# Fewer, longer loads of q and v in an attention kernel, and its bias tiles asked for by GpSimd

## The chip, the cores and the metric

The kernel runs on one core of a Trainium2 chip. What counts is the time of one execution in microseconds of that core (device time); the median of the runs shown is compared. The engines are named as in the profile: PE is TensorE, PEld its weight loads, DVE VectorE, ACT ScalarE, POOL GpSimd, SP SyncE. SP computes nothing: in this kernel it issues the DMAs.

## What is computed

Attention over 4 batches, 8 heads, 576 rows and 64 columns a head, with a bias that a small network makes of the distance of query and key; then a mixture of 8 experts over the 2304 rows, each row with a weight from a Sinkhorn normalization:

```
scores = q @ k.T / sqrt(64) + bias[head]         # bias = relu(x @ w1 + b1) @ w2, x from the positions alone
attn   = softmax(scores)                          # with 1e-9 added to the sum
x      = attn @ v                                 # (4, 8, 576, 64), laid out as 2304 rows x 512
P      = exp(x @ w_gate), 8 times normalized over rows and columns
out    = sum over e of P[:, e] * (relu(x @ w1[e]) @ w2[e])     # 8 experts, 512 -> 1024 -> 512
```

## The kernel before

**Units.** The attention is cut into 16 units: one batch and two heads each (`units`, line 687; neighbouring batches run through the head pairs in opposite order, so that a unit may take over its neighbour's bias tiles). A unit's 576 rows are seen as 64 partitions of `R` = 9 rows each: row 9p + r lies with partition p. Query tiles t = 0 to 3 hold rows r = t and r = t + 4 (128 queries), tile 4 holds row 8 of both heads. A unit has five steps (`unit_steps`): two query tiles for each of two heads, then the next two, then tile 4.

**Loading a unit.** `u_load` asks for q in three DMAs (rows 0 to 3 into partitions 0 to 63, rows 4 to 7 into partitions 64 to 127, row 8 by itself) and for k in one. `u_vload` asks for v in four. All land in the rotating buffers `nat` (four). `u_cut` splits q and k into two f16 halves on ACT and DVE (`asplit`: ACT writes the high part, DVE the rest), `u_trans` turns them on PE into the bank `l1` and evacuates them into `qkT` by ACT, DVE and ACT; GpSimd then writes a copy with the partition halves swapped. `u_v` splits v into `vs`, and GpSimd writes its swapped copy. `b_load` asks for two bias tiles `bt` a unit, unless the unit before has the same heads.

**A step.** PE multiplies q and k into a score bank (`s`, two of them); DVE adds the bias, keeps the row's extreme and frees the bank (`sb`, the custom instruction); ACT takes the exponential (`sb<-sb,st`), then writes the high f16 half of the probabilities into `ah` (two buffers); DVE writes the low half; SP issues a DMA transpose of `ah` into `aT`; PE multiplies `aT` with `vs` (`pv`). Between these, PE works through pieces of expert 0 (`run_piece`, bank `l`).

**Order.** Within the attention every call is recorded (`Plan.record`), with a modelled cost, and what it reads and writes; `Plan.emit` replays the model and emits the instructions in the order of its start times. Each engine then works its own instructions off in that order; SP and GpSimd too. An instruction that waits holds up what stands behind it on its engine. For a DMA on SP the model takes 0.5 us of issuing, on GpSimd 1.05 (`Engine.transfer`, line 224). The steps loop `for n in range(NS + LAG + 1)` at line 1137 calls the loads some steps ahead through `hooks`. Behind the attention come gate, Sinkhorn and experts 1 to 7 (line 1194 on), planned by a second plan.

Of the kernel before, what the change touches and what calls it, by code (L numbers as in the profile page):

```python
# [10 lines left out]
F32 = mybir.dt.float32  # L11
# [7 lines left out]
P = 128  # L19
B, H, S, D = 4, 8, 576, 64  # L20
# [5 lines left out]
R = S // 64  # L26
# [244 lines left out]
def attention_sinkhorn_moe(ctx, tc, q, k, v, w1, b1, w2, wg, m1, m2, xm, xm4, xf, sel, out):  # L271
# [12 lines left out]
    vec, act, pool, pe, sync = (  # L284
        Engine(plan, e, n)
        for e, n in ((nc.vector, "dve"), (nc.scalar, "act"), (nc.gpsimd, "pool"), (nc.tensor, "pe"), (nc.sync, "dma"))
    )
# [62 lines left out]
    sc_bias = dram.tile([H, P, 2, S], F32, name="sc_bias")  # L350
# [62 lines left out]
    with ExitStack() as actx:  # L413
# [21 lines left out]
        nat, spl, uni, bst, wrk = places("nat", 4), places("spl"), places("uni", 2), places("bst", 2), places("wrk")  # L435
# [13 lines left out]
        def ps_s():  # L449
            return psA.tile([P, 1024], F32, name="ps_s", tag="s", bufs=2)  # L450
# [68 lines left out]
        for kind in range(1, 4):  # L519
            vec.scalar_tensor_tensor(  # L520
                out=wr,
# [8 lines left out]
            out=wa.rearrange("p g (j k) -> p (g j) k", j=4),  # L530
# [92 lines left out]
        def bias_step(between=()):  # L623
# [27 lines left out]
            out=w1r, in0=pw[:, H : H + 2], scalar1=s_wb[:, 0:1], scalar2=2.0**-11, op0=ALU.mult, op1=ALU.mult  # L651
# [5 lines left out]
            out=w2m,  # L657
# [22 lines left out]
        for i in range(2):  # L680
            r = slice(32 * i, 32 * i + 1)
# [5 lines left out]
        units = [(b, hp if b % 2 == 0 else NHP - 1 - hp) for b in range(B) for hp in range(NHP)]  # L687
        U = {}

        def nat_tile():  # L690
            return nat.tile([P, 10 * D], F32, name="nat", tag="nat")

        def ld(u):
            return sync

        def u_load(u):
            if u >= len(units):
                return
            b, hp = units[u]
            h0 = 2 * hp  # L700
            qn = nat_tile()[:, : R * D].rearrange("p (r d) -> p r d", d=D)
            src = q[b, h0 : h0 + 2].rearrange("h (p r) d -> p h r d", r=R)
            for i in range(2):
                hs = slice(64 * i, 64 * i + 64)
                ld(u).dma_start(
                    out=qn[hs, 0:8, :].rearrange("p (h c) d -> p h c d", h=2), in_=src[:, :, 4 * i : 4 * i + 4, :]
                )
            ld(u).dma_start(out=qn[:, 8, :], in_=q[b, h0 : h0 + 2].rearrange("h (p r) d -> (h p) r d", r=R)[:, 8, :])
            kn = nat_tile()[:, : R * D].rearrange("p (r d) -> p r d", d=D)
            ld(u).dma_start(out=kn, in_=k[b, h0 : h0 + 2].rearrange("h (p r) d -> (h p) r d", r=R))  # L710
            U[u] = dict(qn=qn, kn=kn)

        def u_cut(u):
# [9 lines left out]
        def u_vload(u):  # L723
            if u >= len(units):
                return
            b, hp = units[u]
            h0 = 2 * hp
            vn = nat_tile().rearrange("p (h c d) -> p h c d", h=2, c=5)
            vv = v[b, h0 : h0 + 2].rearrange("h (p r) d -> p h r d", r=R)
            for i in range(2):  # L730
                hs = slice(64 * i, 64 * i + 64)
                ld(u).dma_start(out=vn[hs, :, 0:4, :], in_=vv[:, :, 4 * i : 4 * i + 4, :])
                ld(u).dma_start(out=vn[hs, :, 4, :], in_=vv[:, :, 8, :])
            U[u]["vn"] = vn

        def u_v(u):
            if u >= len(units):
# [15 lines left out]
        def u_trans(u):  # L753
            if u >= len(units):
                return
            st = U[u]
            if u in (2, 3):
                qkT = xc[:, u - 2, : 27 * P].rearrange("p (n x) -> p n x", x=P)
            else:
                qkT = uni.tile([P, 27, P], F16, name="qkT", tag="qkT")  # L760
            qk = st.pop("qk").rearrange("p (i r) a d -> p i r (a d)", i=2)
            for i in range(3):
                ps = psA.tile([P, 1024], F16, name="ps_t", tag="l1", bufs=2).rearrange("p (r x) -> p r x", x=P)
                rows = [(i, r) for r in range(8)] if i < 2 else [(0, 8), (1, 8)]
                with plan.as_one():
                    for j, (a, r) in enumerate(rows):
                        pe.transpose(ps[:, j], qk[:, a, r], id16)
                if i == 0:
                    act.copy(qkT[:, 0:8], ps)
                elif i == 1:  # L770
                    vec.tensor_copy(qkT[:, R : R + 8], ps)
                else:
                    act.copy(qkT[:, : 2 * R].rearrange("p (i r) x -> p i r x", i=2)[:, :, 8], ps[:, 0:2])
            for i in range(2):
                pool.tensor_copy(qkT[64 * i : 64 * i + 64, 2 * R :], qkT[64 - 64 * i : 128 - 64 * i, :R])
            st.update(q=(qkT[:, :R], qkT[:, 2 * R :]), kT=qkT[:, R : 2 * R])

        def b_load(u, hh):

            if u and units[u][1] == units[u - 1][1]:  # L780
                U[u]["b", hh] = U[u - 1]["b", hh]
                return
            bt = bst.tile([P, 2, S], F32, name="bt", tag="bt")
            sync.dma_start(out=bt, in_=sc_bias[2 * units[u][1] + hh])
            U[u]["b", hh] = bt

        def b_tile(u, t, hh):
# [7 lines left out]
        for n in range(8):  # L795
            for m in (2 * n, 2 * n + 1):
                nm, _, i = qk_order[m]
# [9 lines left out]
        with plan.urgent():  # L807
# [6 lines left out]
            out=c8, in0=u_qk[:, 0:1], scalar=0.125, in1=u_qk[:, 1:2], op0=ALU.mult, op1=ALU.mult  # L814
# [7 lines left out]
            out=g, in0=g0, scalar=s_qk[:, 0:1], in1=s_qk[:, 1:2], op0=ALU.mult, op1=ALU.mult  # L822
# [25 lines left out]
        with plan.urgent():  # L848
            u_cut(0)
            u_trans(0)  # L850
# [49 lines left out]
        def scores(u, t, hh):  # L900
            ps = ps_s()
            kT = U[u]["kT"]
            kv = kT[:, 0:8, :].rearrange("p (r c) x -> p c r x", r=2)
            for a, qT in enumerate(U[u]["q"]):
                for c in range(2):
                    for h in (hh,) if t < 4 else (0, 1):
                        hs = slice(h * 64, h * 64 + 64)
                        lhs = qT[:, 4 * h + t, :] if t < 4 else qT[:, 8, hs]
                        rhs = kT[:, 8, hs] if c else kv[:, :, :, hs]
                        o = (ps if t < 4 else ps[hs])[:, 512 * c : 512 + 64 * c]  # L910
                        pe.matmul(o, lhs, rhs, start=(a == 0), stop=(a == 1))
            return ps
# [224 lines left out]
        for n in range(NS + LAG + 1):  # L1137
# [19 lines left out]
            if 0 < n <= NS:  # L1157
# [3 lines left out]
                u, gi, hh = s["key"]  # L1161
# [24 lines left out]
        vec, act, pool, pe, sync = nc.vector, nc.scalar, nc.gpsimd, nc.tensor, nc.sync  # L1186
# [41 lines left out]
    h0 = box["h"]  # L1228
# [552 lines left out]
    for e in range(1, E):  # L1781
        a, b = (x for x in (1, 2, 3) if x != here)
# [86 lines left out]
    for n, (e, b) in enumerate(seq):  # L1869
        r = visit[n]  # L1870
        i, at_end, leaves = (b, r % 2), n % 5 == 4, visit[n + 1 : n + 2] != [r]
# [31 lines left out]
def _constants():  # L1903
    import numpy as np

    pos = np.arange(S)
    rel = (pos[:, None] - pos[None, :]).astype(np.float32)
    x = np.log1p(np.abs(rel)) / np.log1p(np.maximum(pos[:, None].astype(np.float32), np.float32(1.0)))
    x = x.astype(np.float32)
    x4 = x * np.float32(4.0)  # L1910
    hi = x4.astype(np.float16)
    lo = (x4 - hi.astype(np.float32)).astype(np.float16)
    p = np.arange(64)
    half = lambda r: 9 * p + r
    key = np.concatenate([half(c + 4 * r) for c in range(4) for r in range(2)] + [half(8)])
    tiles = [np.concatenate([half(t), half(t + 4)]) for t in range(4)] + [half(8)]
    res, xf = [], []
    for tk in tiles:
        xr = x[np.ix_(tk, key)]
        if len(tk) == P:  # L1920
            xf.append(xr)
        else:
            half_keys = np.concatenate([xr[:, : S // 2], xr[:, S // 2 :]])
            xf.append(np.concatenate([half_keys, 0 * half_keys], axis=1))
        a = np.zeros((4, XR // 4, 36, len(tk)), np.float16)
        for part, src in enumerate((hi, hi, lo, lo)):
            g = src[np.ix_(tk, key)].reshape(len(tk), 36, 4, 4)
            if len(tk) < P:
                g = g.reshape(len(tk), 2, 18, 4, 4).transpose(0, 2, 1, 3, 4).reshape(len(tk), 36, 4, 4)
            a[:, 4 * part : 4 * part + 4] = g.transpose(2, 3, 1, 0)  # L1930
        a[:, 16:18] = 4.0
        res.append(a.reshape(XR, -1))
    sel = np.zeros((128, 24), np.float32)
    for g in range(4):
        for r in range(18):
            sel[18 * g + r, r // 4 % 2 if r < 16 else r - 14] = 1.0
            sel[18 * g + r, 8 + 4 * g + np.arange(4)] = [float(r >= 16 or r % 4 == j) for j in range(4)]
        sel[32 * g : 32 * g + 32, 4 + g] = 1.0
    return np.stack(res[:4]), res[4], np.stack(xf), sel
# [28 lines left out]
```

## Time and profile before

| | |
|---|---|
| runs: median, lowest, highest | 1784.96, 1783.5, 1785.4 us |
| the profiled execution's own time | 1784.56 us |
| its span, first to last instruction | 1782.8 us |
| PE, DVE, ACT, POOL busy in the span | 1686.8, 1447.8, 1086.3, 78.7 us |
| HBM traffic over the span | 156 GB/s |

The profile is of one execution. Its page gives shares of the whole span, over stages that have different limits: the preparation of the bias and the first units (to about 200 us), the attention proper (to about 505 us), then gate and experts. Busy time of PE holds weight loads apart. A row of waits names the instruction that waited and what it waited for last. The time of a DMA row on SP is that of its issuing; when its data has landed is seen only by who waited for it.

### The profile page before, as it was taken

The numbers are of one execution on the slowest core, as the hardware profiler recorded it, in microseconds if no ns is written. First come the engines' busy times: TensorE is split into PE (matmuls) and PEld (weight loads), VectorE is DVE, ScalarE is ACT, GpSimd is POOL, SyncE is SP. The second block draws the span as 40 slices with busy tenths as digits, with TensorE's granted clock in tenths as the row PEclk, the third lists the DMA queues.
The fourth block names the chain that finished last, engine by engine and source line by source line (L and its number), as shares of the span: only waits on it lengthen the run. The fifth ranks groups of instructions, "written<-read, shape, count | busy, mean of one in ns | idle before, by whom it ended". The sixth has DMA issues, their size and how long they took to land.

```text
span 1782.8 us, 40479 instructions
## 1 busy us (share of the span) xinstructions
PE 1686.8 (95%) x16640; PEld 1377.4 (77%) x16640; DVE 1447.8 (81%) x2627; ACT 1086.3 (61%) x1930; POOL 78.7 (4%) x90
## 2 busy tenths in 40 slices
PE   7887897898989999999999999999999999999998
PEld 4544564555666688888988898889888988898887
DVE  6898988898968898778887787878788878876666
ACT  7887888888856675545564555565555544453443
POOL 0120012122200000000000000000000000000000
PEclk9988799999999999999999999999999999999999
DMA  7769999999993164644473557445545653463321
GB/s 259 240 160 225 206 196 200 200 201 194 202 268 136 68 204 181 231 165 163 170 279 135 201 190 248 154 143 213 214 173 180 237 192 131 160 238 103 104 73 37
DMA packets 303358, 324.24 MB, mean 182 GB/s; under 512 B 191420, under 2 KB 231876, under 8 KB 298180
## 3 DMA queue, kind: packets, MB, share of 16 engines
q1 hardware_dynamic: 303172, 321.65, 60.0%
q8 instruction: 130, 2.13, 0.5%
q14 instruction: 56, 0.46, 0.1%
HBM read 189.86 MB, written 88.08 MB: 156 GB/s over the span
## 4 chain that ended last, share of the span: by engine, by line
PE 78%; DVE 8%; DMA 7%; ACT 3%; issue 2%; SPq 0%; DVEq 0%; ACTq 0%
PE bankA L1591 18%; PE bankA L1611 13%; PE bankE L1591 9%; PE bankE L1611 9%; PE bankB L1611 9%; PE l L210 6%; PE bankB L1591 4%; DMA aT<-ah 4%; PE s L210 4%; PE pv L210 3%; ACT area L210 2%; DVE ah L210 1%; DVE area L210 1%; DVE sb L210 1%; PE bankS L1427 1%
## 5 line engine op out<-in xcount | busy, mean ns | idle before, releaser
L1591 PEld LDWEIGHTS <-slot 128*128 128x128 f16 x5040 | 450.7, 98 | 48.3 <-issue 2.5
L1611 PEld LDWEIGHTS <-hA 128*128 128x128 f16 x2268 | 222.4, 98 | 27.1 <-issue 0.6
L210 PEld LDWEIGHTS <-area 128*128 128x128 f16 (+1 forms) x2477 | 155.2, 101 | 101.5 <-issue 33.2
L1591 PE MATMUL bankA<-xt,slot 128*128 128x256 f16 (+1 forms) x1680 | 186.1, 262 | 0.2 <-ACT u L1648 0.2
L1591 PE MATMUL bankE<-xt,slot 128*128 128x256 f16 (+1 forms) x1680 | 186.1, 262 | 0.0
L1636 ACT ACTIVATE hA<-c 128x512 f16<-128x512 f32 x189 | 118.0, 627 | 111.3 <-DVE c L1214 110.4
L1611 PEld LDWEIGHTS <-hS 128*128 128x128 f16 x1512 | 147.2, 98 | 22.2 <-ACT hS L1636 3.0
L1611 PEld LDWEIGHTS <-area 128*128 128x128 f16 x1512 | 148.0, 98 | 18.5 <-issue 1.4
L210 DVE SCALAR_TENSOR_TENSOR ah<-sb,st,ah 128x576 f16<-128x576 f32 x144 | 122.4, 876 | 24.1 <-ACT ah L210 23.9
L1214 DVE SCALAR_TENSOR_TENSOR hA<-c,hA 128x512 f16<-128x512 f32 x189 | 127.5, 685 | 12.3 <-ACT hA L1636 10.2
L1695 ACT COPY u<-bankA 128x512 f32<-128x512 f32 (+1 forms) x70 | 37.8, 540 | 157.6 <-PE bankA L1611 157.4
L210 ACT ACTIVATE ah<-sb,st 128x576 f16<-128x576 f32 x144 | 106.2, 770 | 37.6 <-DMA aT<-ah 33.5
L1648 ACT ACTIVATE u<-bankA 128x512 f32<-128x512 f32 x126 | 75.1, 596 | 67.6 <-PE bankA L1591 63.8
L210 ACT ACTIVATE sb<-sb,st 128x576 f32<-128x576 f32 x144 | 110.4, 769 | 7.4 <-DVE st L210 7.1
L210 PE MATMUL l<-area 128*128 128x512 f16 (+1 forms) x413 | 110.6, 385 | 3.5 <-ACT ys L210 0.4
L1214 DVE SCALAR_TENSOR_TENSOR acc<-c,fs,acc 128x256 f32<-128x256 f32 x252 | 110.6, 480 | 2.1 <-DMA out_dram<-acc 0.2
L210 PE MATMUL s<-qkT 128*128 128x512 f16 (+3 forms) x560 | 84.5, 302 | 23.0 <-DVE st L210 22.1
L1611 PE MATMUL bankA<-area,hS 128*128 128x256 f16 x756 | 88.6, 273 | 3.2 <-ACT hS L1636 2.5
L1611 PE MATMUL bankA<-area,hA 128*128 128x256 f16 x756 | 89.8, 276 | 0.0
L1611 PE MATMUL bankA<-area 128*128 128x256 f16 x756 | 88.2, 273 | 1.0 <-ACT u L1695 1.0
L1611 PE MATMUL bankE<-area,hS 128*128 128x256 f16 x756 | 88.5, 273 | 0.0
L1611 PE MATMUL bankB<-area,hA 128*128 128x256 f16 x756 | 88.2, 273 | 0.0
(239 smaller groups left out, 3155.6 us busy)
## 6 DMA issues: line engine op xcount, KB each, us to landing
sc_w<-stage SPq DMA_DIRECT2D x84, 512.0 KB
acc<-sc_y SPq DMA_DIRECT2D x102, 256.0 KB
area<-sc_w SPq DMA_DIRECT2D x48, 512.0 KB
sc_y<-acc SPq DMA_DIRECT2D x84, 256.0 KB
xt<-sc_t SPq DMA_DIRECT2D x18, 1024.0 KB
slot<-sc_w SPq DMA_DIRECT2D x36, 512.0 KB
bt<-sc_bias SPq DMA_DIRECT2D x26, 576.0 KB
raw<-in_moe_w_dram SPq DMA_DIRECT2D x28, 512.0 KB
```

The lines of the kernel that those rows point to most:

```text
L210: self.plan.record(self.name, cost, lambda: fn(*args, **kw), ins, outs, move)
L1214: vec.scalar_tensor_tensor(out=o, in0=x, scalar=s, in1=y, op0=op0, op1=op1)
L1427: pe.matmul(r, id16 if sg > 0 else nid16, v[:, a, 2 * dq : 2 * dq + 2, tok * w : tok * w + w], start=(j == 0), stop=(j == len(seq_) - 1),)
L1591: pe.matmul(ps[:, jf * w : jf * w + w], t[:, a, c * 512 + f * P : c * 512 + f * P + P], x(xp, c), start=(first and jf == 0 and c == 0 and ...
L1611: pe.matmul(ps[:, j * 256 : j * 256 + 256], h[:, a, fc * w + j * P : fc * w + j * P + P], t[:, wp, fc * 256 : fc * 256 + 256], start=(firs ...
L1636: on_act(0.58, lambda: act.activation(h[:, 0, sl], x, AF.Relu if relu else AF.Copy), [r], wk)
L1648: on_act(0.55, lambda: act.activation(tmp[k], bank[b], f, scale=HS), [b], [k], 0)
L1695: on_act(0.27 * nt, lambda: act.copy(tmp[k][:, :n], bank[b][:, :n]), [b], [k], 0)
```

## The change

q of a unit is loaded as k is, by one DMA of 128 partitions x 2304 bytes: a partition now holds nine rows of one head. The halves are put in their places in the evacuation behind the transposes, by a permuted view on ACT. v comes by two DMAs, rows 0 to 4 into partitions 0 to 63 and rows 5 to 8 into partitions 64 to 127, into a buffer of its own (`vnat`, a single one, whose unused part is cleared once); `nat` has three buffers, for q and k alone. The keys' order follows v's: chunk c now pairs rows c and c + 5, and the last chunk is row 4 in place of row 8 (`_constants`, `scores`, `kv`). The bias tiles of the attention are asked for by `pool.dma_start` in place of `sync.dma_start`. What is computed and the bytes read stay the same.

```diff
         def nat_tile():
-            return nat.tile([P, 10 * D], F32, name="nat", tag="nat")
-
-        def ld(u):
-            return sync
+            return nat.tile([P, R * D], F32, name="nat", tag="nat", bufs=3).rearrange("p (r d) -> p r d", d=D)
+
+        vnat = nat.tile([P, 10 * D], F32, name="vnat", tag="vnat", bufs=1).rearrange("p (h c d) -> p h c d", h=2, c=5)
+        pool.memset(vnat[64:128, :, 4, :], 0.0)
...
-            qn = nat_tile()[:, : R * D].rearrange("p (r d) -> p r d", d=D)
-            src = q[b, h0 : h0 + 2].rearrange("h (p r) d -> p h r d", r=R)
-            for i in range(2):
-                hs = slice(64 * i, 64 * i + 64)
-                ld(u).dma_start(
-                    out=qn[hs, 0:8, :].rearrange("p (h c) d -> p h c d", h=2), in_=src[:, :, 4 * i : 4 * i + 4, :]
-                )
-            ld(u).dma_start(out=qn[:, 8, :], in_=q[b, h0 : h0 + 2].rearrange("h (p r) d -> (h p) r d", r=R)[:, 8, :])
-            kn = nat_tile()[:, : R * D].rearrange("p (r d) -> p r d", d=D)
-            ld(u).dma_start(out=kn, in_=k[b, h0 : h0 + 2].rearrange("h (p r) d -> (h p) r d", r=R))
+            qn, kn = nat_tile(), nat_tile()
+            for o, x in ((qn, q), (kn, k)):
+                sync.dma_start(out=o, in_=x[b, h0 : h0 + 2].rearrange("h (p r) d -> (h p) r d", r=R))
...
-            vn = nat_tile().rearrange("p (h c d) -> p h c d", h=2, c=5)
             vv = v[b, h0 : h0 + 2].rearrange("h (p r) d -> p h r d", r=R)
-            for i in range(2):
-                hs = slice(64 * i, 64 * i + 64)
-                ld(u).dma_start(out=vn[hs, :, 0:4, :], in_=vv[:, :, 4 * i : 4 * i + 4, :])
-                ld(u).dma_start(out=vn[hs, :, 4, :], in_=vv[:, :, 8, :])
-            U[u]["vn"] = vn
+            sync.dma_start(out=vnat[0:64], in_=vv[:, :, 0:5, :])
+            sync.dma_start(out=vnat[64:128, :, 0:4, :], in_=vv[:, :, 5:9, :])
+            U[u]["vn"] = vnat
...
                 if i == 0:
-                    act.copy(qkT[:, 0:8], ps)
+                    act.copy(
+                        qkT[:, 0:8].rearrange("p (h t) (i x) -> p h t i x", h=2, i=2),
+                        ps.rearrange("p (i t) (h x) -> p h t i x", i=2, h=2),
+                    )
...
-            st.update(q=(qkT[:, :R], qkT[:, 2 * R :]), kT=qkT[:, R : 2 * R])
+            kv = qkT[:, R : 2 * R + 1].rearrange("p (r c) x -> p c r x", r=2)
+            st.update(q=(qkT[:, :R], qkT[:, 2 * R :]), kT=qkT[:, R : 2 * R], kv=kv)
...
-            sync.dma_start(out=bt, in_=sc_bias[2 * units[u][1] + hh])
+            pool.dma_start(out=bt, in_=sc_bias[2 * units[u][1] + hh])
...
-            kv = kT[:, 0:8, :].rearrange("p (r c) x -> p c r x", r=2)
+            kv = U[u]["kv"]
...
-                        rhs = kT[:, 8, hs] if c else kv[:, :, :, hs]
+                        rhs = kT[:, 4, hs] if c else kv[:, :4, :, hs]
...
-    key = np.concatenate([half(c + 4 * r) for c in range(4) for r in range(2)] + [half(8)])
+    key = np.concatenate([half(c + 5 * r) for c in range(4) for r in range(2)] + [half(4)])
```

Where this puts the issues is the planner's work. SP's queue in the attention proper, from the 28th to the 30th transpose, before (`nat` is q, k or v by its source, `ys` a result of expert 0):

```order
L210 DMA_TRANSPOSE aT_138<-ah_144 128x18x128
L210 DMA sc_y<-ys_108 128x512
L210 DMA nat_119<-in_q_dram 128x64
L210 DMA nat_120<-in_k_dram 128x576
L210 DMA nat_127<-in_v_dram 64x2x256
L210 DMA_TRANSPOSE aT_122<-ah_142 128x18x128
L210 DMA_TRANSPOSE aT_0_117<-ah_144 128x9x128
L210 DMA bt_121<-sc_bias 128x1152
L210 DMA nat_127<-in_v_dram 64x2x64
L210 DMA sc_y<-ys_108 128x512
```

The same place of SP's queue after the change:

```order
L210 DMA_TRANSPOSE aT_138<-ah_144 128x18x128
L210 DMA sc_y<-ys_108 128x512
L210 DMA nat_128<-in_k_dram 128x576
L210 DMA nat_120<-in_q_dram 128x576
L210 DMA_TRANSPOSE aT_123<-ah_142 128x18x128
L210 DMA_TRANSPOSE aT_0_118<-ah_144 128x9x128
L210 DMA sc_y<-ys_108 128x512
```

Pieces of v and the bias tile are gone from between these transposes; k and q stand as one row each.

GpSimd's queue after the change, in the first units with bias tiles asked for there (before, only the copies of `vs` and `qkT` stand here, in the same order):

```order
L210 DMA bt_122<-sc_bias 128x1152
L210 COPY vs_145<-vs_145 64x640
L210 COPY vs_145<-vs_145 64x2x256
L210 DMA bt_124<-sc_bias 128x1152
L210 COPY vs_145<-vs_145 64x2x64
L210 COPY qkT_127<-qkT_127 64x1152 x2
L210 DMA bt_122<-sc_bias 128x1152
L210 COPY qkT_129<-qkT_129 64x1152 x2
L210 DMA bt_124<-sc_bias 128x1152
```

The bias tiles moved in between the copies, each of which now stands behind a bias tile's wait for its buffer.

SP's queue at the end of the preparation, from the fifth to the seventh transpose, after the change (`br` is bias work, `area<-in_moe_w` are weights of expert 0):

```order
L210 DMA_TRANSPOSE aT_138<-ah_142 128x18x128
L210 DMA br_111<-area 64x4x128 x2
L210 DMA vnat_116<-in_v_dram 64x2x320
L210 DMA vnat_116<-in_v_dram 64x2x256
L210 DMA br_111<-area 64x4x128 x2
L210 DMA area<-in_moe_w_dram 128x2x512
L210 DMA br_111<-area 64x4x128 x2
L210 DMA_TRANSPOSE aT_123<-ah_144 128x18x128
L210 DMA br_111<-area 64x4x128 x2
L210 DMA area<-in_moe_w_dram 128x2x512
```

Before, two bias issues stood ahead of the fifth transpose, one pair of `br` between the fifth and the sixth, and all weights behind the sixth.

## Rows read from the trace of the kernel before

**Rows 1.** The page: busy time of each engine.
```profile
PE 1686.8 (95%) x16640; PEld 1377.4 (77%) x16640; DVE 1447.8 (81%) x2627; ACT 1086.3 (61%) x1930; POOL 78.7 (4%) x90
```

**Rows 2.** Stretches: busy PE, PEld, DVE, ACT, POOL; PE's granted clock, DMA share, GB/s.
```profile
100.00:200.00 100.00, 77.61 (x939) 48.19 (x936) 87.95 (x194) 77.86 (x153) 10.65 (x14) 0.85 0.86 207
200.00:300.00 100.00, 89.36 (x874) 56.66 (x873) 88.26 (x196) 82.52 (x166) 18.60 (x20) 0.95 0.93 198
300.00:400.00 100.00, 88.38 (x878) 57.25 (x872) 89.23 (x200) 83.46 (x169) 20.31 (x20) 0.95 0.99 199
400.00:505.00 105.00, 95.21 (x946) 60.02 (x945) 91.75 (x203) 87.06 (x179) 20.36 (x20) 1.00 0.90 189
```

**Rows 3.** Waits, 205 to 505 us: who, for whom, us in total, times, longest.
```profile
ACT ah L210 <- DMA aT<-ah: 24.0, 23, 2.2
...
DVE ah L210 <- ACT ah L210: 21.3, 22, 2.5
PE s L210 <- DVE st L210: 19.4, 24, 2.1
```

**Rows 4.** Issues by tile, SP: count, ns least/median/most, first and last start, us.
```profile
L210 SPq DMA_TRANSPOSE aT<-ah x80: 1253/3078/6224, 94.2 to 509.4; - x80
...
L210 SPq DMA_DIRECT2D nat<-in_v_dram x64: 595/607/1930, 69.8 to 469.0; - x64
L210 SPq DMA_DIRECT2D nat<-in_q_dram x48: 357/602/1607, 42.1 to 441.2; - x48
...
L210 SPq DMA_DIRECT2D nat<-in_k_dram x16: 327/420/607, 44.2 to 446.6; - x16
...
L210 SPq DMA_DIRECT2D bt<-sc_bias x26: 338/524/618, 147.7 to 474.7; - x26
```

**Rows 5.** SP in order of time: start, duration, what. 279 to 286 us.
```profile
279.74 0.65 SPq L210 DMA_DIRECT2D nat<-in_v_dram  x1
280.50 4.85 SPq L210 DMA_TRANSPOSE aT<-ah  x2
```

**Rows 6.** DVE and ACT there, in order of time; idle before it in brackets.
```profile
278.24 0.81 DVE L210 SCALAR_TENSOR_TENSOR ah<-sb,st,ah 128x576 f16<-128x576 f32 x1
...
285.90 1.44 ACT L210 ACTIVATE ah<-sb,st 128x576 f16<-128x576 f32 x2 [1.79 <-DMA aT<-ah]
```

**Rows 7.** SP, DVE and ACT in order of time, 409 to 418 us.
```profile
410.65 1.30 SPq L210 DMA_DIRECT2D nat<-in_v_dram  x2
412.07 3.68 SPq L210 DMA_TRANSPOSE aT<-ah  x1
...
409.19 1.54 DVE L210 SCALAR_TENSOR_TENSOR ah<-sb,st,ah 128x576 f16<-128x576 f32 x2
...
417.81 0.78 ACT L210 ACTIVATE ah<-sb,st 128x576 f16<-128x576 f32 x1 [0.92 <-DMA aT<-ah]
```

**Rows 8.** SP in order of time: a transpose behind a bias tile, one alone.
```profile
200.76 0.52 SPq L210 DMA_DIRECT2D bt<-sc_bias  x1
...
202.56 3.68 SPq L210 DMA_TRANSPOSE aT<-ah  x1
...
215.82 2.70 SPq L210 DMA_TRANSPOSE aT<-ah  x1
```

**Rows 9.** DVE beside GpSimd, in order of time; DVE's `ah` by line, 205 to 505 us.
```profile
307.11 2.43 DVE L210 SCALAR_TENSOR_TENSOR ah<-sb,st,ah 128x576 f16<-128x576 f32 x2 [1.12 <-ACT ah L210]
...
306.00 2.94 POOL L210 COPY qkT<-qkT 64x1152 f16<-64x1152 f16 x2 [11.96 <-ACT qkT L210]
...
L210 DVE SCALAR_TENSOR_TENSOR ah<-sb,st,ah 128x576 f16<-128x576 f32 x118 | 101.6, 891 | 21.5 <-ACT ah L210 21.3
```

**Rows 10.** DVE in order of time: last and first reads of a bias buffer.
```profile
198.94 0.81 DVE L210 CUSTOM_DVE_ANT_0 sb<-s,bt,sms 128x576 f32<-128x576 f32 x1
...
206.80 0.81 DVE L210 CUSTOM_DVE_ANT_0 sb<-s,bt,sms 128x576 f32<-128x576 f32 x1
```

## The prediction

> **What bounds the kernel now.** I read the page first, then a table by stretch, then the waits of the attention, then the SyncE queue row by row. The page has TensorE (PE) busy for 95% of the span [rows 1]: whatever is gained must come out of the rest, or out of stretches with a lowered clock. By stretch, PE idles 10.6, 11.6 and 9.8 us in the three from 200 to 505 us, where attention units 4 to 15 run, with the granted clock at 0.95, 0.95 and 1.00 of its upper level, 2.4 GHz [rows 2]. There VectorE is busy for 87 to 89% and the DMA packets sum to 0.90 to 0.99 of 16 engines. So no one engine is the bound; four queues run close to full and wait for one another in turn.
>
> The waits between 205 and 505 us show the turn [rows 3]. ScalarE waits 24.0 us, 23 times, before it writes `ah`, until a transpose out of `ah` has landed (`ah` has two buffers). VectorE then waits 21.3 us for ScalarE's `ah`, and PE 19.4 us for the score bank that VectorE reads. A transpose that lands late is what starts this row of waits. When it starts is SyncE's affair: each transpose takes SyncE 3.08 us (median), each load of a piece of q or v 0.60, of k 0.42, of a bias tile 0.52 [rows 4]. One unit (four large transposes, one half as long at 1.25, three q, one k, four v, 26 bias tiles over 16 units) thus takes SyncE about 12.3 + 1.3 + 1.8 + 0.4 + 2.4 + 0.9 = 19.1 us. From the transpose at 280.50 to the one at 412.07 there are 29 steps of transposes, five a unit, so a unit lasts 131.57 / 5.8 = 22.7 us [rows 5, 7]: SyncE's queue is some 84% full.
>
> **Part 1: q by one transfer, v by two.** It removes two of three q issues and two of four v issues a unit, 64 in all, 38.6 us of SyncE's time; the q that stays should go as k does now, 0.42 for 0.60. What a unit's loads take falls from 5.5 us (1.8 + 0.4 + 2.4 + 0.9, bias tiles with them) to 2 x 0.42 + 2 x 0.61 = 2.1, by 63%. Bytes stay the same, so I take nothing for the DMA engines.
>
> Only the time in which a ready transpose stood behind such a load counts. Take the wait of 1.79 us at 285.90: its transpose was issued at 280.50, right behind a v load (279.74 to 280.39), while VectorE's last `ah` of it ended at 279.05 [rows 5, 6]. At 417.81 ScalarE waits 0.92 us; the transpose was issued at 412.07 behind two v loads, with VectorE's `ah` done at 410.73 [rows 7]. I went so through the 23 waits: in 11 of them (first 259.97, last 468.76) loads stood between a finished `ah` and its transpose. Counting no more than the wait itself, the loads' share is 5.4 us. The other transposes started within 0.1 us of their `ah` and were late for reasons that the change leaves alone: the 2.7 us that one takes SyncE even when nothing is ahead (at 215.82) and the landing [rows 8]. Of 5.4 us, 63% goes: **3.4 us**. Bounds: nothing (VectorE, freed, meets the next wait) and all 24.0 us.
>
> **Part 2: the bias tiles go to GpSimd.** SyncE loses 26 x 0.524 = 13.6 us of issuing, counted above. A transpose right behind a bias tile took 3.68 us at 202.56, against 2.70 at 215.82 [rows 8]. Three of the 23 waits (208.17, 244.92, 431.51) have a tile just ahead of their transpose; with at most 1 us each that is 2.9 us. The tile still moves its 576 KB over the same 16 engines at nearly the same time, so I take half: **1.5 us**, bounds 0 and 2.9. The Trainium skill, "DMA: Bandwidth & Descriptors", section "Issuing engines are not separate DMA queues", says that transfers started by different engines interleave on the same 16 engines and that only the issue time is saved; by it this term would be 0 and the sum 1.5 us smaller.
>
> What is added is 26 issues on GpSimd, whose price the trace doesn't show. Below, SyncE's 0.52 us; above, 1.47 us, one of the two GpSimd copies of `qkT` at 306.00 [rows 9]. GpSimd is busy 78.7 us in the whole span [rows 1], so I take its own queue at nothing. Queued behind a waiting bias issue are the copies of `vs` and `qkT`; GpSimd itself idled before nearly all of these. Ahead of it stand copies that in the trace of before end in time: if I set each bias issue at the later of the last read of its buffer and the copy that now precedes it, the tightest tile is asked for at 199.75 (the read of 198.94 ends) and first read at 206.80 [rows 10]; only three of 26 have less than 13 us, and before, the tightest had 6.0 (issued at 200.76 [rows 8]).
>
> GpSimd's work is not free for VectorE, though. Two `ah` passes take 1.54 us alone [rows 7] and took 2.43 at 307.11, while GpSimd copied `qkT` from 306.00 to 308.94; the mean of 118 such passes is 891 ns, over the 0.81 of the one at 278.24 [rows 6, 9]. Per bias issue the loss of VectorE lies between 0 and 0.89 us. Issuing a DMA reads no tile, unlike a copy, so I take 0 and keep 0.89 for a rival.
>
> **Part 3: order of keys, one `vnat` buffer, three `nat`.** The q evacuation on ScalarE writes the same 1024 columns from a permuted PSUM view; the scores read keys in runs of 64 as before: nothing. With one `vnat` the next v load waits for both passes over the last v, a unit earlier, so nothing from unit 4 on; for units 1 to 3 the loads move behind each other in SyncE's queue. The planner lays the whole order out anew: before the seventh transpose two bias issues are gone and two v pieces and one expert weight have moved ahead of the sixth. PE idles 22.4 us between 100 and 200 us at a clock of 0.85 [rows 2], so this can go either way; I take 0, with 4 us either side.
>
> **Sum.** 3.4 + 1.5 = 4.9 us off the profiled execution's 1784.56, of which 1782.8 is the span: 1779.7. The median of the runs is 0.4 above that execution: **1780 us**.
>
> **Rivals.** (A) *The loads were hidden.* For it: in 12 of the 23 waits no load stood before the transpose, and VectorE at 87 to 89% has little room [rows 2]. A transpose that starts 1 us earlier then only waits later. Time 1784.6 plus or minus 3. (B) *The queue frees more than the sum.* Transposes also queue behind transposes that were late; if two thirds of ScalarE's 24.0 us go, and PE follows, 16 us: about 1769. Against it: VectorE would need 93% of those stretches. (C) *GpSimd's issuing holds VectorE.* Place: `ah` and `vs` passes from 205 us on. At half of the measured 0.89, 0.45 us x 26 = 11.6 us, less the 4.9 gained: 1784.6 + 6.7 = 1791 (at the full 0.89, 1803). It turns the kernel slower by over 0.2% once a bias issue costs VectorE more than (4.9 + 3.6) / 26 = 0.33 us. For it: the copies at 306.00; against: a descriptor is no tile. (D) *A bias tile comes late.* An issue that is held up by eight or more passes of 0.81 us eats the 7 us of slack of the tightest tile; if it hits all, 26 x 2 us = 52, so 1837. The Trainium skill, "SBUF — State Buffer", section "SBUF: two separate sides", speaks for it: a DMA asked for by GpSimd can't get its descriptors written while VectorE runs an op in a two-port mode. No row of before shows such a DMA. (E) *The new order is worse in the first 200 us*, up to the 4 us above and the gain not reached: 1789.
>
> **How the numbers follow.** 3.6 us, 0.2%, is about what a measurement of this kernel can tell from no change. Chances: the forecast (3.6 to 9 us off) 0.36, B 0.12, A 0.31, C 0.13, E 0.06, D 0.02. So faster 0.48, same 0.31, slower 0.21. The range reaches from B to C, 1769 to 1791; beyond are D and the ends of B and C. Cases of one sign, with A beside them, hold most of the chance, so it needs no second range.
>
> **What would show it.** Right: q rows of SyncE at about 0.42 us, 16 of them; ScalarE's wait for `aT` below 24 us, near 18, and VectorE's for `ah` with it; transposes starting within 0.1 us of their `ah` oftener; VectorE's `ah` mean at 891 ns still [rows 9]. Wrong: that wait unchanged (A); an `ah` mean well above 891, or GpSimd rows of over 1.5 us for a bias tile (C); VectorE or its `sb` pass waiting for `bt` (D); PE idle above 22.4 us between 100 and 200 us (E).

## The result: slower, and what the profile after shows

The changed kernel takes 1795.07 us (median of six runs, 1791.8 to 1803.6), the kernel before 1784.87 on the same chip: a ratio of 1.0061, 95% interval 1.0044 to 1.0077. The forecast was 1780. The profiled execution of after took 1793.91 us, its span 1791.9.

The page's busy time, beside [rows 1]. PE's work is the same; the span's 9.1 us more are time in which it waits or runs at a lower clock.

```profile
PE 1688.3 (94%) x16640; PEld 1378.1 (77%) x16640; DVE 1442.6 (81%) x2627; ACT 1087.8 (61%) x1930; POOL 92.8 (5%) x117
```

The stretches of [rows 2], same columns. PE idles 27.0 us between 100 and 200 us where it idled 22.4, and 14.4 where it idled 11.6 between 300 and 400.

```profile
100.00:200.00 100.00, 73.00 (x855) 43.83 (x854) 84.01 (x188) 74.10 (x146) 15.33 (x21) 0.84 0.88 208
200.00:300.00 100.00, 89.56 (x884) 57.50 (x883) 85.54 (x181) 80.72 (x162) 23.39 (x27) 0.94 0.89 183
300.00:400.00 100.00, 85.64 (x858) 56.28 (x859) 88.94 (x207) 84.16 (x170) 22.35 (x28) 0.95 1.00 204
400.00:505.00 105.00, 97.35 (x966) 61.78 (x961) 89.65 (x207) 86.95 (x179) 21.93 (x26) 0.98 0.91 185
```

The waits from 205 to 505 us, beside [rows 3]. ScalarE's wait for a transpose is 22.7 us, hardly less than the 24.0 of before, and its longest is now 3.6 where it was 2.2. GpSimd's own wait at a tile's buffer is long, but no row names anybody who waits for `bt`.

```profile
POOL bt L210 <- DVE st L210: 106.3, 9, 15.1
...
ACT ah L210 <- DMA aT<-ah: 22.7, 19, 3.6
DVE ah L210 <- ACT ah L210: 21.3, 23, 3.2
PE s L210 <- DVE st L210: 18.8, 15, 2.9
```

The issues, beside [rows 4] (SyncE's by tile, then GpSimd's of `bt`, with the time from issue to landing). The change does in SyncE's queue what it says: 16 rows of q in place of 48, at 428 ns in place of 602, 32 of v in place of 64.

```profile
L210 SPq DMA_TRANSPOSE aT<-ah x80: 1272/2923/5177, 92.2 to 515.6; - x80
...
L210 SPq DMA_DIRECT2D nat<-in_q_dram x16: 328/428/1116, 42.1 to 422.8; - x16
...
L210 SPq DMA_DIRECT2D nat<-in_k_dram x16: 328/468/593, 42.6 to 445.5; - x16
...
L210 SPq DMA_DIRECT2D vnat<-in_v_dram x32: 595/618/758, 67.9 to 468.5; - x32
...
L210 POOL DMA_DIRECT2D bt<-sc_bias x26: 527/527/667, 146.2 to 484.6; - x26
...
DMA to landing us min/median/max: 3.9/5.8/9.5
```

Where the time went is told best by when a given transpose starts (SyncE's queue in order of time). I take the 15th, at the end of the preparation, and the last, the 80th; between them lie the same 65 steps in every kernel. These times are of one execution of each kernel, and executions of one kernel lie some microseconds apart.

| kernel | 15th starts | 80th starts | between | end of the span after the 80th |
|---|---|---|---|---|
| before | 210.55 | 509.44 | 298.89 | 1273.3 |
| after | 213.67 | 515.61 | 301.94 | 1276.3 |

So 3.1 us are lost in the first 210 us, 3.1 in the attention, where a gain was forecast, and 3.0 behind it.

One place of the first part: tiles are asked for by GpSimd at 183.17 and 186.44, the second while the transpose that began at 184.88 is still being issued (the second of the four in the SyncE row; it took 4.68 us). By the packet records the first tile moves from 186.18 to 189.06, the second from 190.51 to 195.41. ScalarE's `ah` waits 1.75 us, until 188.80, and 2.44 us, until 196.20, and in its queue the cuts of expert 0's weights (`area`) stand behind. The last such cut on VectorE starts at 215.88 us, in the trace of before at 207.53. Whether these tiles or the new order made the cuts late is settled further down, in the square. First SyncE and GpSimd, then ScalarE, in order of time:

```profile
182.15 19.15 SPq L210 DMA_TRANSPOSE aT<-ah  x4
```

```profile
183.17 0.53 POOL L210 DMA_DIRECT2D bt<-sc_bias  x1 [17.42 <-DVE st L210]
186.44 0.53 POOL L210 DMA_DIRECT2D bt<-sc_bias  x1 [2.75 <-DVE st L210]
```

```profile
188.80 0.77 ACT L210 ACTIVATE ah<-sb,st 128x576 f16<-128x576 f32 x1 [1.75 <-DMA aT<-ah]
189.48 1.13 ACT L210 ACTIVATE area<-area,sms 128x1024 f16<-128x1024 f32 x1
...
196.20 2.11 ACT L210 ACTIVATE ah<-sb,st 128x576 f16<-128x576 f32 x3 [2.44 <-DMA aT<-ah]
198.21 1.13 ACT L210 ACTIVATE area<-area,sms 128x1024 f16<-128x1024 f32 x1
```

### The profile page after: what moved, and what is told of

The parts are those of the page before. It is cut to its first block, busy times and chain, and to the rows that moved or that the text cites. A ratio compares the mean times of both kernels' runs of the same rounds, so it can differ in the third digit from the quotient of the medians.

```text
span 1791.9 us, 40397 instructions
## 1 busy us (share of the span) xinstructions
PE 1688.3 (94%) x16640; PEld 1378.1 (77%) x16640; DVE 1442.6 (81%) x2627; ACT 1087.8 (61%) x1930; POOL 92.8 (5%) x117
## 4 chain that ended last, share of the span: by engine, by line
PE 76%; DMA 10%; DVE 8%; ACT 3%; issue 2%; SPq 0%; DVEq 0%; ACTq 0%
PE bankA L1585 18%; PE bankA L1605 13%; PE bankE L1585 9%; PE bankE L1605 9%; PE bankB L1605 9%; DMA aT<-ah 6%; PE l L210 5%; PE bankB L1585 4%; PE s L210 4%; PE pv L210 3%; ACT area L210 2%; DVE ah L210 1%; DMA br<-area 1%; PE bankS L1421 1%; DVE area L210 1%
## 5 line engine op out<-in xcount | busy, mean ns | idle before, releaser
L210 PE MATMUL pv<-aT,vs 128*64 128x256 f16 (+3 forms) x1176 | 77.7, 267 | 11.4 <-DMA aT<-ah 9.0
```

The costliest lines, as they stand in the source:

```text
L210: self.plan.record(self.name, cost, lambda: fn(*args, **kw), ins, outs, move)
```

## The experiments

Each ratio is to runs of the kernel before that were taken beside the run in question (medians 1784.6 to 1785.4 us).

**Theory 1:** a bias tile that GpSimd asks for no longer stands in line with the transposes. Its packets run beside theirs, the transposes land later, and what waits for them is late. **Rival 2:** the order of the work, which the planner laid out anew, is to blame. **Rival 3:** the q and v part itself, its single `vnat` buffer above all. **Rival 4:** GpSimd's way of asking costs something whenever it is done.

### The two parts apart

The whole change, with the bias tiles on SyncE again (their order is planned for SyncE too):

```diff
-            pool.dma_start(out=bt, in_=sc_bias[2 * units[u][1] + hh])
+            sync.dma_start(out=bt, in_=sc_bias[2 * units[u][1] + hh])
```

> The whole change, but the bias tiles of the attention are asked for by SyncE again. Theory 1 (bias tiles on GpSimd start as soon as a buffer is free and slow the transposes between 160 and 200 us): the loss goes, 1780 to 1785 us, and the 20th transpose starts near 239 us as before (after: 244). Rival 2 (the new planned order of the q, v and key part is to blame): still 1790 or more, expert 0's weight cuts still some 8 us late. Rival 3 (a single buffer for v makes loads late): also 1790 or more.

1779.34 us (1777.6 to 1784.3), ratio 0.9965 (0.9953 to 0.9978): faster than before, as theory 1 has it, just below its range. Rival 3 falls. Its waits from 205 to 505 us are near what was forecast for the change (18 us for the first):

```profile
ACT ah L210 <- DMA aT<-ah: 18.8, 18, 2.4
PE s L210 <- DVE st L210: 17.6, 19, 2.9
DVE ah L210 <- ACT ah L210: 16.7, 18, 2.7
```

The kernel before, with the tiles on GpSimd and nothing else changed in the source. The planner lays the order out anew here too (SyncE's queue differs from about 152 us on, where the bias tiles begin), so this run holds the queue and an order of its own:

```diff
-            sync.dma_start(out=bt, in_=sc_bias[2 * units[u][1] + hh])
+            pool.dma_start(out=bt, in_=sc_bias[2 * units[u][1] + hh])
```

> The kernel before, with nothing changed but that the attention's bias tiles are asked for by GpSimd. Theory 1: 1789 to 1795 us, with the loss of 5 us or more between 160 and 230 us. Rivals 2 and 3 (loads and order of q, k and v are to blame): 1783 to 1786 us, as before.

1833.49 us (1831.8 to 1837.6), ratio 1.0274 (1.0249 to 1.0299). The sign is theory 1's, the size is far beyond it: the bias part alone, with its order, costs 49 us, more than the whole change. Its waits name the transposes:

```profile
POOL bt L210 <- DVE st L210: 119.9, 11, 21.8
...
ACT ah L210 <- DMA aT<-ah: 48.0, 21, 9.4
DVE ah L210 <- ACT ah L210: 35.9, 23, 7.5
PE pv L210 <- DMA aT<-ah: 32.9, 9, 7.3
```

Five places carry most of it; here is the one at 371 us. SyncE begins a transpose at 370.98, GpSimd asks for a tile at 371.33, 0.35 us later:

```profile
370.98 2.61 SPq L210 DMA_TRANSPOSE aT<-ah  x1
...
375.57 7.33 SPq L210 DMA_TRANSPOSE aT<-ah  x1
```

```profile
371.33 0.53 POOL L210 DMA_DIRECT2D bt<-sc_bias  x1
```

In the chain of waits of this stretch the transpose takes 10.94 us (the longest of the chain of before, from 205 to 505 us, takes 6.29):

```profile
370.98 10.94 DMA aT<-ah
```

And in the table of stretches (columns as in [rows 2]) the packets of the slow piece take more of the engines' time than those ahead of it, and move less: 126 GB/s at a share of 1.21, where it was 169 at 0.96 (and 199 at 0.99 before the change between 300 and 400 us [rows 2]). PE stands, and its clock falls to 0.50, the lower of its two levels, 1.2 GHz.

```profile
368.00:371.00 3.00, 3.00 (x40) 2.44 (x37) 2.97 (x5) 2.80 (x7) 2.94 (x3) 1.00 0.96 169
...
373.60:381.00 7.40, 2.09 (x13) 0.83 (x11) 4.10 (x8) 2.66 (x5) 0.00 (x0) 0.90 1.21 126
381.00:384.00 3.00, 2.04 (x17) 1.53 (x16) 1.17 (x2) 1.44 (x2) 0.00 (x0) 0.50 1.17 294
```

The trace's packet records tell whose packets these are. A tile is 128 packets of 4608 bytes, a large transpose 2304 of 256 bytes. This tile's packets run from 373.61 to 380.91, with 1302 packets of 256 bytes between them that take 66 ns on average; away from all tiles (over 1 us, 205 to 505 us) such a packet takes 23 (median 18).

### Order and queue as a square

Two more kernels take order and queue apart. The first has the planner's order for tiles on SyncE, but GpSimd asks for them; the second the other way round. (`Engine`'s last word is the name under which the planner counts.)

```diff
+    gpq = Engine(plan, nc.gpsimd, "dma")
-            pool.dma_start(out=bt, in_=sc_bias[2 * units[u][1] + hh])
+            gpq.dma_start(out=bt, in_=sc_bias[2 * units[u][1] + hh])
```

> The whole change, the bias tiles asked for by GpSimd, but the order of all other work is laid out as if they stood in SyncE's queue (the order of the kernel with q, v and keys alone). Theory 1 (what counts is when the tiles start): 1790 to 1795 us, as the whole change. Rival 2 (the order that the planner makes when it charges GpSimd for them): as the kernel with q, v and keys alone, within 2 us.

```diff
+    spq = Engine(plan, nc.sync, "pool")
-            pool.dma_start(out=bt, in_=sc_bias[2 * units[u][1] + hh])
+            spq.dma_start(out=bt, in_=sc_bias[2 * units[u][1] + hh])
```

> The whole change in its own planned order (laid out as if GpSimd asked for the bias tiles), but SyncE asks for them: the fourth corner beside q, v and keys alone (1779.3), its order with the tiles on GpSimd (1790.4) and the whole change (1795.1). If queue and order add up: 1779.3 + (1795.1 - 1790.4) = 1784.0, so 1782 to 1786. If the queue alone counts (theory 1): 1778 to 1781. If the order of the change is the main loss (rival 2): 1790 or more.

| | order planned for tiles on SyncE | order planned for tiles on GpSimd |
|---|---|---|
| SyncE asks | 1779.34 | 1784.53 (0.9999, 0.9989 to 1.0009) |
| GpSimd asks | 1790.36 (1.0030, 1.0012 to 1.0048) | 1795.07 (1.0061, 1.0044 to 1.0077) |

Down a column, VectorE, ScalarE, GpSimd and SyncE have the same sequence of instructions in the traces to the end of the attention, the tiles' issues apart. The queue costs 11.0 us in one order and 10.5 in the other; the order costs 5.2 and 4.7. By the intervals each of these differences is uncertain by 3 to 4 us; within that they add up. The change's result is then -5.3 us for q, v and keys, 5.2 for the order and 10.5 for the queue (this sum follows the corners of the square, so it comes out by itself). The queue carries some two thirds of the loss, the order, rival 2, some one third.

That the queue's part goes by the transposes, as theory 1 has it, is seen in ScalarE's wait for them from 205 to 505 us, at a fixed order. In the order for tiles on SyncE it is 18.8 us (shown above) with SyncE asking, and with GpSimd asking:

```profile
ACT ah L210 <- DMA aT<-ah: 30.0, 18, 4.3
```

In the order for tiles on GpSimd it is 22.7 us in after (shown above), and with SyncE asking:

```profile
ACT ah L210 <- DMA aT<-ah: 12.9, 17, 1.7
```

So 11.2 and 9.8 us more, close to what the queue costs. The chain of waits of the same stretch, shares by line, agrees. First the order of after with SyncE asking, then after:

```profile
by line: PE l L210 27.4%; DMA aT<-ah 17.5%; PE pv L210 11.0%; PE s L210 10.3%; DVE ah L210 9.3%; issue 5.5%; DVE sb L210 5.0%; ACT ah L210 3.8%; DVE area L210 2.0%; ACT sb L210 1.9%; DVE qk L210 1.5%; DVE st L210 0.9%; DVE vs L210 0.7%; ACT
```

```profile
by line: DMA aT<-ah 28.4%; PE l L210 25.5%; PE pv L210 12.5%; PE s L210 9.3%; DVE ah L210 6.9%; issue 4.4%; ACT ah L210 3.8%; DVE sb L210 2.7%; DVE qk L210 1.3%; ACT sb L210 1.1%; DVE area L210 1.1%; DVE vs L210 0.6%; DVE st L210 0.6%; ACT
```

A transpose on its way (`DMA aT<-ah`) holds 17.5% of the chain with the tiles in SyncE's queue, and 28.4% with the tiles on GpSimd (14.2 and 26.4% in the other order). The longest takes 7.0 us and 8.6 (6.5 and 10.7).

The late start of after, on the other hand, is the order's: with SyncE asking in that order the 15th transpose starts at 213.79 (213.67 in after) and the last weight cut at 214.02 (215.88), though ScalarE's `ah` has no wait at 190 and 196 us there. So the tiles at 183 and 186 us may account for some of the last cut, not for the late start.

### Some of the tiles

```diff
-            pool.dma_start(out=bt, in_=sc_bias[2 * units[u][1] + hh])
+            (sync if u < 4 else pool).dma_start(out=bt, in_=sc_bias[2 * units[u][1] + hh])
```

> The whole change, but the bias tiles of units 0 to 3 (asked for up to some 200 us) stay with SyncE, the others go to GpSimd. Theory 1 (early collisions cost 5 to 7 us, and the rest of the attention even gains 1 to 2): 1784 to 1789 us. If the bias tiles of the later units cost as much, 1790 or more. Rival 3 (a single buffer for v): 1790 or more.

1787.80 us (1780.0 to 1797.2), ratio 1.0009 (0.9987 to 1.0031). The counterpart has `pool if u < 4 else sync`:

> The whole change, but only the bias tiles of units 0 to 3 are asked for by GpSimd, the others by SyncE: the counterpart of the run in which these four were on SyncE (1787.8). If what the tiles cost adds up from single meetings: 1779.3 + (1795.1 - 1787.8) = 1786.6, so 1784 to 1789 us. If only the steady attention pays: 1778 to 1782 us.

1787.36 us (1783.5 to 1789.7), ratio 1.0008 (0.9996 to 1.0020), 0.8 us from the sum. So, order and queue together, the early tiles cost 7.3 us (1795.07 - 1787.80) to 8.0 (1787.36 - 1779.34), the later ones 7.7 to 8.5, each uncertain by some 4 us. That the loss sits in the early ones alone and the rest of the attention gains, as theory 1 had it for the first of these runs, is wrong.

### The moment, and another queue

In the kernel with the bias part alone, added work ahead of each tile: GpSimd clears the buffer first.

```diff
+    class Late:
+        def dma_start(self, out, in_):
+            nc.gpsimd.memset(out, 0.0)
+            nc.gpsimd.dma_start(out=out, in_=in_)
+    gpq = Engine(plan, Late(), "pool")
```

> The kernel before with its bias tiles asked for by GpSimd (1833 us), and ahead of each such issue GpSimd clears the tile's buffer, which the transfer then overwrites: some 2 us of added work on GpSimd for each of 26 tiles, all else in the same order. Theory 1, as the traces now put it (five tiles are asked for 0.35 us after a transpose of SyncE has begun; their packets and the transpose's take turns, and both are through only 7.3 to 9.1 us later, where other tiles take 2.3 to 3.6): those five now start about 2 us later and none takes over 5 us, so 1785 to 1800 us. Rival 4 (GpSimd's way of asking costs by itself, whenever it is done): 1830 us or more, since the work was only added to.

1799.78 us (1795.2 to 1803.3): 33.7 us faster with 26 operations of 1.06 us more. One tile still takes 6.21 us, no other over 4.03. Rival 4 falls as the main cause: what a tile costs depends on the moment in which it is asked for. The 14.4 us that are left over before are not told apart; the order, the added work and other meetings share them.

```profile
L291 POOL MEMSET bt<- x26: 1051/1057/1077, 134.9 to 493.6; 128x1152 f32 x26
```

```profile
ACT ah L210 <- DMA aT<-ah: 25.9, 17, 4.1
```

Then the whole change with ScalarE asking for the tiles, the rest in the order for SyncE:

```diff
+    gpq = Engine(plan, nc.scalar, "dma")
```

> The whole change, the order of all other work as with the tiles on SyncE, but ScalarE asks for the bias tiles. Theory 1 (what counts is that a tile no longer stands in one queue with the transposes): a tile's packets still take 3 us and more where they meet a transpose, and 1786 to 1796 us. Rival 4 (only GpSimd's way of asking does it): tiles take 2.6 us as from SyncE, and 1778 to 1784 us, 26 issues of 0.5 us on ScalarE being the only price.

1786.85 us (1784.8 to 1789.5), ratio 1.0015 (1.0005 to 1.0024): the time that theory 1 expected, but not by its mechanism. Tiles took 2.43 us on average and at most 4.14, and its 65 steps from the 15th to the 80th transpose take 292.96 us, as with SyncE (292.54). In the profiled execution its loss lies ahead of the 15th (215.05 for 211.27) and behind the 80th (1277.9 us for 1271.9). So a second queue need not cost the attention anything; this run speaks for neither side alone.

So I forced the moment: the 18 tiles of units 4 to 15 are asked for right behind the next large transpose, once by GpSimd, once by ScalarE, each after copying one element that VectorE's last `ah` pass has written.

```diff
+        def dma_start_transpose(self, out, in_):
+            nc.sync.dma_start_transpose(out=out, in_=in_)
+            while held and in_.free_size() > 1152:
+                o, s = held.pop(0)
+                nc.gpsimd.tensor_copy(out=o[:, 0, 0:1], in_=in_[:, in_.free_size() - 1 :])
+                nc.gpsimd.dma_start(out=o, in_=s)
```

> The q, v and key part with the order of all else as in its own run (1779.3 us), but the 18 bias tiles of units 4 to 15 are asked for by GpSimd right when the next transpose of 18 blocks begins: ahead of each issue GpSimd copies one element that this transpose also waits for. If the phase is the cause (a tile asked for some 0.35 us after a transpose has begun): most of the 18 tiles take over 6 us, and at the 6.7 us for each that the run with later tiles gave back (33.7 / 5) some 1840 to 1900 us. If the five slow tiles had another cause: no tile over 5 us and 1785 to 1800.

1811.05 us (1795.8 to 1820.6), ratio 1.0165 (1.0114 to 1.0216). Slower by 31.7 us than the same tiles in SyncE's queue, but short of the forecast, and the profiled execution (1795.8) has three slow tiles of 18 (4.57, 5.44, 6.18 us), not most. Its tiles were asked for 0.48 us and more after the transpose began, none at 0.35. That tiles came late is not the reason: nothing that reads a tile waits for one from 205 us on.

> The same, with ScalarE in GpSimd's place: same moment, same order, another queue and way of asking. If any second queue in this phase does it: tiles over 6 us, 1840 us or more. If only GpSimd's way of asking does it: no tile over 4 us; ScalarE's own wait for VectorE's last pass ahead of each issue costs up to 18 x 1.5 us, so 1780 to 1810 us.

1804.96 us (1802.6 to 1814.6), ratio 1.0123 (1.0089 to 1.0157). The profiled execution is the slowest of its four (1814.6). Three of 18 tiles are slow in it as well: 5.42, 6.22 and 11.67 us. The time alone would fit the second line of the expectation; the rows decide for the first, in kind though not in size: in this phase a queue that GpSimd has no part in has slow tiles too. The chain of this stretch has the longest transpose of all runs:

```profile
467.85 18.80 DMA aT<-ah
```

All tiles from 175 us on, in all kernels of this case, by how many 256-byte packets ran between a tile's first and last packet (counted from the packet records; from the kernels that load q or v by 256 bytes a few of these are theirs). The tiles with 100 to 400 such packets are left out: 46, 35 and 11 for the three queues, 2.55, 2.69 and 2.57 us on average.

| queue | 256-byte packets beside | tiles | mean us | longest | ns a 256-byte packet |
|---|---|---|---|---|---|
| SyncE, with the transposes | up to 100 | 78 | 2.54 | 4.56 | 18 |
| | 400 to 699 | 30 | 2.82 | 3.91 | 40 |
| | 700 and more | 0 | | | |
| GpSimd | up to 100 | 35 | 2.59 | 3.36 | 22 |
| | 400 to 699 | 47 | 3.28 | 5.58 | 44 |
| | 700 and more | 12 | 6.17 | 9.07 | 57 |
| ScalarE | up to 100 | 13 | 2.01 | 2.52 | 21 |
| | 400 to 699 | 13 | 2.80 | 3.92 | 33 |
| | 700 and more | 5 | 6.16 | 11.67 | 59 |

In the transposes' own queue a tile never had more than 700 such packets beside it. From another queue it can have up to 2000, and then tile and transposes are slow together, whoever asks (6.17 and 6.16 us). A tile that is slow has more packets beside it for that reason alone, so the table tells that slow tiles and transposes go together, not which slows which. Nor does it say how often: 12 of GpSimd's 129 tiles are in the last group, and all 5 of ScalarE's 42 come from the run with the forced moment.

### q and v apart

The kernel before with q by one transfer, and the kernel before with v by two, its buffer and the new keys:

> The kernel before, with q alone by one transfer a unit (v in four, keys and bias tiles as before). If the gain of the q and v part (5.3 us) goes by SyncE's time (q 1.4 us a unit of the 2.6 that q and v lose): 1781 to 1783 us. If it is all in q's transfers: 1779 to 1780. If it is all in v's, or in the new order of the keys: 1784 to 1785.

> The kernel before, with v by two transfers into its own buffer and the new order of the keys; q in three transfers, bias tiles on SyncE. Since q alone gave nothing (1785.3 beside 1785.4 of before): 1779 to 1781 us if v's part carries the 5.3 us by itself, 1782 to 1785 if SyncE's time has to fall by both for the transposes to profit.

| kernel | us, ratio to before | 15th starts | 15th to 80th | ScalarE's wait for `aT`, 205 to 505 |
|---|---|---|---|---|
| before | | 210.55 | 298.89 | 24.0 |
| q alone | 1785.27, 1.0010 (0.9998 to 1.0021) | 213.87 | 296.40 | 20.9 |
| v alone | 1787.68, 1.0015 (1.0001 to 1.0029) | 215.02 | 295.55 | 17.4 |
| q, v and keys | 1779.34, 0.9965 (0.9953 to 0.9978) | 211.27 | 292.54 | 18.8 |

Neither part alone makes the kernel faster, and v alone is above what was expected for it. Yet in the attention of the profiled executions the gains add up: 2.5 and 3.3 us, together 6.35. What differs is the first 210 us, where each new order starts the 15th transpose 3.3, 4.5 and 0.7 us later than before.

## Why the prediction was wrong, step by step

**Part 1, right in the attention, its size small.** Loads ahead of ready transposes do hold the attention up. Between 205 and 505 us 33 of 65 transposes started within 0.1 us of VectorE's last `ah` pass before; it is 43 of 67 with q, v and keys alone and 43 of 64 in after. Forecast were 3.4 us, which took the tiles' issues as gone too; for q and v alone the same working gives 5.4 x 2.5 / 5.5 = 2.5. The attention gains 6.35, the kernel 5.3. How much of that is the luck of the order that came with it is not shown: q alone and v alone gain in the attention and nothing in the whole. q's rows stand at 428 ns, sixteen of them, as forecast.

**Part 2, the step that failed.** "I take half: 1.5 us, bounds 0 and 2.9" is 10.5 to 11.0 us on the other side. I had read the transpose of 3.68 us behind a tile [rows 8] as a price of the tile standing in SyncE's queue, to be saved by moving it. That row was one pair: over all large transposes of before between 205 and 505 us the issue takes 3.6 us behind a tile (11 of them) and 3.1 otherwise. Nor is it saved: it takes 3.30 on average in after, where no tile stands in that queue, and 3.20 before. Tile and transposes still meet on the 16 engines; what SyncE's queue gave was that they overlapped less (never over 700 packets beside a tile). For the added issues I priced GpSimd's and VectorE's time and set nothing for the transposes already on their way; no bound contained it. The Trainium skill's rule weighed there ("DMA: Bandwidth & Descriptors", section "Issuing engines are not separate DMA queues"), by which the term would be 0, was nearer than mine: it has transfers of different askers interleave on the same engines, and the packet records agree. That only the issue time is saved, they don't bear out: the interleaving has a price, here seven times the 1.5 us.

**Part 3 and E, the price near, the chance too small, the place in part.** Between the two planned orders lie 4.7 to 5.2 us (the square), just over the 4 us kept for a new order. PE idles 27.0 us between 100 and 200 us, above the 22.4 named as its sign, and 26.2 in the same order with SyncE asking, so the sign goes with the order. But of the 10.3 us between the profiled executions of the two orders with SyncE asking (their medians are 5.2 apart) only 2.5 lie ahead of the 15th transpose, 4.8 in the 65 steps and 2.9 behind them: the first 200 us, E's place, hold a part of it. In every kernel of this study the 15th transpose of the profiled execution starts later than before, by 0.7 to 8.7 us; I gave that case 0.06.

**The other rivals.** A is refuted by the run with q, v and keys alone, and B (1769) came in no run. C is refuted: VectorE's `ah` mean fell, in the grouped row that answers to [rows 9],

```profile
L210 DVE SCALAR_TENSOR_TENSOR ah<-sb,st,ah 128x576 f16<-128x576 f32 x114 | 95.3, 867 | 21.3 <-ACT ah L210 21.3
```

and D did not come: from 205 to 505 us no row of after has anybody waiting for a tile. Both looked at GpSimd's side of the issue; the price was on the side of the transposes. What I offered as a sign for success, ScalarE's wait for `aT` near 18 us, came true in the kernel without the bias part (18.8) and not in after (22.7), which tells the two parts apart in one row. It is no measure of the time by itself: with v alone it is 17.4 and in the order of after with SyncE asking 12.9, and neither kernel is faster than before.

**What stays open.** Why some meetings of tile and transpose go slow and others don't. All five tiles asked for 0.35 us after a transpose in the bias part alone were slow; of 36 that were tied to a transpose on purpose, six. With GpSimd clearing first, the slow one was asked for 0.30 us after; but from ScalarE a tile asked for at 0.38 took 2.78 us, and six at 0.18 to 0.19 took 2.4 to 4.0. So the phase alone does not decide. And why the order for tiles on GpSimd costs some 5 us: the late weight cuts of expert 0 (last one at 214.02 us in that order with SyncE asking, 206.46 in the other) are seen, but were not moved back alone.

The kernel to keep is the change without its last line: q, v and keys, with the bias tiles on SyncE, 1779.34 us, faster than both.

## What to carry to other kernels

A queue is also an order: taking a bulk load out of the queue of latency-bound transfers saves its issue and gives up that the two pass one after the other, so price what the load does to transfers already on their way before you price the issue. Measure the parts of a change apart, and where a planner lays everything out anew, measure its order apart too (same order, other queue, and the reverse): here a gain of 5.3 us was hidden under two losses. When the time between two marks of the steady stage and the time of the whole kernel disagree, look ahead of the first mark and behind the second: in after, 3.1 us were lost ahead and 3.0 behind.

## What the runs showed of the hardware

- Two streams on the same 16 DMA engines from different queues can be slower together than one after the other. The tile at 373.61 and the 1302 packets beside it took 7.3 us; an estimate for one after the other is 2.5 us for a tile with few packets beside it and 1302 x 23 ns / 16 = 1.9, together 4.4. The stretch moved 126 GB/s at a DMA share of 1.21, the one just before 169 at 0.96. A 256-byte packet takes 23 ns on average away from tiles and 57 to 59 in such meetings. The Trainium skill, "DMA: Bandwidth & Descriptors", section "Queues, rings and completion order", says that an engine takes turns between queues by packets; packets of both kinds run in the same stretch, as that would have it, but the records don't name a packet's engine. Why a packet itself takes more than twice as long stays open.
- A tile asked for by GpSimd while SyncE issues a transpose mostly starts to move only when that issue has ended: asked for at 371.33, its first packet runs at 373.61, and the transpose's issue ended at 370.98 + 2.61 = 373.59. Of 100 such tiles in all runs, 95 had their first packet behind the end of the issue and five ahead of it, by 0.38 us at most. The lag from asking to the first packet is 2.5 us there (median), and 1.4 with no transpose being issued. A tile of ScalarE's started 3.20 us ahead of such an end, so it is no rule for every second queue.
- One late transpose costs PE twice: it stands, and the granted clock is 0.50 from 381 to 384 us, when the work is back.
